# A fused S4D convolution and gated unit: eight pace units less ahead of the chunks, 4.4 per chunk, and transfers moved between queues

## The chip, the cores and the metric

The kernel runs on one core of one Trainium2 chip. A core has a matrix engine (TensorE, PE in the profile), a vector engine (DVE), a scalar engine (ACT), GpSimd (POOL) and SyncE (SP), each with its own list of instructions that it works off in order, and 16 DMA engines that all queues share. The metric is the device time of one execution in microseconds; a version's time is the median of its runs.

## The reference

The input u has 2048 tokens of 448 values. It is normalised once, and the result goes two ways; their sum with u is the output:

```python
xn = layernorm(u)
# state space convolution
A = -exp(log_A_real) + 1j * A_imag          # 448 x 256 modes
P = exp((A * dt[:, None])[:, :, None] * pos)
K = 2.0 * einsum("dn,dnl->dl", C * dt, P).real
y = irfft(rfft(xn.T, 2 * L) * rfft(K, 2 * L))[:, :L].T + xn * D_skip
# gated unit
h = sigmoid(xn @ w_gate) * (xn @ w_up)      # 448 -> 1792
out = u + y + h @ w_down                    # 1792 -> 448
```

All data are float32. The gated unit's matmuls work on values that are split in a high and a low part, so that each product is three matmuls (high by high, high by low, low by high).

## The kernel before, in words

**Two streams.** The program is written by two Python generators that run in turns while it is built: `conv()` for the convolution and `glu()` for the gated unit. Each yields a number of units of work, and the driver at the end of the file always continues the one with the smaller share done of its `total`. The constants at the top are these units: `WP` and `WX` for the preparation, `AHEAD` once before the chunks, `WK` for a chunk (given out in three parts), `HOLE` behind the chunks, `WS` for a step of the spectra. So they set how much of the gated unit is written between two pieces of the convolution. From the first step of the spectra on, the two take strict turns (`turns`) at each yield. A scheduler then places the instructions on the engines' lists, by the order written and by its own model of time; `tc.issue_after(x)` keeps an instruction behind `x`, if both are on the same engine, and does nothing to one on another engine. `sp_mm` and `glu_mm` hold the last matmul of each stream, so that with `issue_after` the matmuls of the spectra and of the gated unit stand on PE in the order in which they were written.

**The convolution.** 56 chunks of 8 channels each make the convolution's kernel K out of the modes. In each, four loads bring a phase table on SP (L483, `ph`), PE spreads it (L533, `tr`), ACT takes the sine of it (L541 to L544, `S`), POOL makes the modes' factors (L511, `me`, `mf`), DVE multiplies (L602 to L604, `Et`, `Ft`), and PE sums over the modes in 64 matmuls (L618, `ko`). Every four chunks a first stage of the transform (L559) goes to a buffer in DRAM (`sk_d`). The first stage of the tokens' own transform goes to DRAM as `x_d` (L279, in `x1_store`).
The spectra are 17 steps. A forward step (`there`, L891) multiplies both first stages by a table on PE into `pk` and `px`; DVE adds and subtracts (L898), multiplies both spectra (`product`), adds again (`halves`, L912), and one turn later PE goes back (`back`, L926), ACT copies the result to `vt`, and DMAs write it to `v_d` and bring it back turned (`turned`, `vp`). `last` (L962) makes the last stage for two halves h of the columns and four quarters q of the tokens, DVE adds it to `acc`, and `out_end` writes finished rows of the output (L232).

**The gated unit.** The tokens are worked in two halves of 1024, each as two blocks t of 512; the 1792 inner columns in 14 blocks, taken in groups of three (two in the last). `gate` makes gate and up projection of one column block and one token block, 11 matmuls `gu` of 512 columns each (L709); ACT takes the tanh (`th`, L717), DVE multiplies (L720), ACT rounds to the high part `hh` (L725) and DVE makes the low part `hl` (L727). After a group, nine matmuls `po` (L812) for each of the four 128-token blocks b give its part of the output, and DVE adds it to `acc` (L817). The first half splits the weights and stores both parts in DRAM, the second loads them back (L771 on SP). In the last group of the first half (`cross`) the tokens of the second half are loaded, normalised and transposed, and `pair_first` makes the first stage of their transform: ACT copies it (L693), and four stores for each pair of token blocks put it into `x_d`. At its end `acc` goes to `acc_d` (L832), and `acc` is loaded afresh with u for the second half (L236, on ACT's queue):

```python
if half == 1:
    for q in (2, 3):
        accs.append(acc_tile())
        x_load(accs[q], 4 * q, 4, [nc.scalar])
```

Of the last group of the second half, the block (t, b) = (0, 1) and all behind it are held back (`yield None`) until the convolution has written its last back step. What is left of `po` then stands between that and the last stage, except for the blocks of t = 1 with b above `LASTS`, which stand behind it.

Of the kernel before, what the change touches and what calls it, by code (L numbers as in the profile page):

```python
# [20 lines left out]
D = 448  # L21
# [5 lines left out]
TWO_PI = 2.0 * math.pi  # L27
MAGIC = 1.5 * 2.0**23
NFT = F // 128
WK = 4.83  # L30
WS = 5
HOLE = 6
AHEAD = 34
WP = 5
WX = 2
HELD = 9
LASTS = 1
HP = 300
Y0 = (8, 1)
CP = D // 4  # L40
# [86 lines left out]
def s4d_glu_kernel(ctx, tc, io):  # L127
    nc = tc.nc
# [556 lines left out]
    def pair_first(b, xns):  # L685

        x1 = pg.tile([128, 2, D], F32, name="x1", tag="wraw", bufs=1)
        pss = [psg.tile([128, 512], F32, name="gu", bufs=4) for _ in range(4)]
        for g in range(4):
            x_first_stage(pss[g][:, :D], xns, g)  # L690
        for g in range(4):
            to = x1[:, g] if g < 2 else pg.tile([128, D], F32, name="x1", tag="rd", bufs=RB)
            nc.scalar.copy(to, pss[g][:, :D])  # L693
            x1_store(row(b, g), to, nc.scalar)

    def gate(w, xs, to, between=None):
        wh, wl = w
# [32 lines left out]
    def glu():  # L730
        stores, later = [], []
        for half in range(2):
            if half == 1:
                for q in (2, 3):
                    accs.append(acc_tile())
                    x_load(accs[q], 4 * q, 4, [nc.scalar])
            for fs_ in ORDER[half]:
                fc, f0 = len(fs_), fs_[0]
                wts, ws, hs = [], [], [[], []]
# [12 lines left out]
                for n_, (f, t) in enumerate(order):  # L752
                    if t == 0:
                        wh = pg.tile([128, 2, 4, 128], F32R, name="wh", bufs=2)
                        if half == 0:
                            first = len(raws) == 2
                            raw, rd = raws.pop()
                            wl = w_low()
                            with hp(HP):
                                nc.scalar.copy(wh, raw)  # L760
                                if first:
                                    v.scalar_tensor_tensor(wl, raw, lim[:, 0, 0:1], wh, ALU.mult, ALU.subtract)
                                else:
                                    v.tensor_tensor(wl, raw, wh, ALU.subtract)
                            if not raws and f + 1 < NFT:
                                raws.append((w_load(f + 1), None))
                            stores.extend(kept((wh, wl), wt_d, f))
                        else:
                            wl = w_low()
                            for t_, d_ in kept((wh, wl), wt_d, f):  # L770
                                nc.sync.dma_start(t_, d_)  # L771
                        ws.append((wh, wl))
                    between = (lambda s_=mid[n_]: step(*s_)) if cross and mid[n_] else None
                    yield from gate(ws[f - f0], xq[2 * half + t], hs[t], between)
                    for t_, d_ in stores:
                        nc.sync.dma_start(d_, t_)
                    stores[:] = later
                    later.clear()
                    if t == 0:
                        dh = pg.tile([128, D], F32R, name="dh", bufs=FCH[0])  # L780
                        if half == 0:
                            rd = rd or rd_load(f)
                            dl = d_low()
                            with hp(HP), tc.issue_after((act if f == 1 else marks)[0].ins):
                                nc.scalar.copy(dh, rd)
                            nc.gpsimd.tensor_tensor(dl, rd, dh, ALU.subtract)
                            later.extend(kept((dh, dl), dt_d, f))
                        else:
                            dl = d_low()
                            for t_, d_ in kept((dh, dl), dt_d, f):  # L790
                                nc.sync.dma_start(t_, d_)
                        wts.append((dh, dl))
                    yield 2.5
                    for s_ in end[n_] if cross else ():
                        step(*s_)
                    if cross:
                        yield 2
                for t in range(2):
                    acc = accs[2 * half + t]
                    for b in range(4):  # L800
                        if final and (t, b) == (0, 1):

                            yield None
                        bs = slice(128 * b, 128 * b + 128)
                        end_ = final and (t, b) == (1, 3)
                        for h, ds in enumerate((slice(0, H), slice(H, D)) if end_ else (slice(0, D),)):
                            po = psg.tile([128, D], F32, name="po", tag="gu", bufs=4)
                            n = 0
                            with tc.issue_after(sp_mm[0].ins) if glu_on else nullcontext():
                                for (hh, hl), (dh, dl) in zip(hs[t], wts):  # L810
                                    for a_, w_ in ((hh, dh), (hh, dl), (hl, dh)):
                                        glu_mm[:] = [nc.tensor.matmul(  # L812
                                            po[:, ds], a_[:, bs], w_[:, ds], start=(n == 0), stop=(n == 3 * fc - 1)
                                        )]
                                        n += 1
                            with hp(HP):
                                v.scalar_tensor_tensor(  # L817
                                    acc[:, b, ds], po[:, ds], 0.5, acc[:, b, ds], ALU.mult, ALU.add
                                )
                            if final and t == 1 and b > 1:  # L820
                                out_end(acc[:, b : b + 1], 12 + b, ds)
                        if final and (t, b) == (1, LASTS):
                            sp_mm[:] = glu_mm
                            for q in range(4):
                                lasts[0](1, q)
                        if final and (t, b) == (1, 1):
                            out_end(acc[:, 0:2], 12, slice(0, D))
                        yield 0.6 * fc
                        if cross and (t, b) in downs:
                            step(*downs[t, b])  # L830
                    if cross:
                        nc.sync.dma_start(acc_d[:, 4 * t : 4 * t + 4], acc)  # L832

    def spectra(pf):
# [119 lines left out]
        def last(h, q):  # L954
# [15 lines left out]
                a = acc[:, p::2, ds]  # L970
                v.tensor_tensor(a, a, half(pb[q % 2][:, p, : 2 * H]), ALU.add)
            if h == 1 and q < 3:
                out_end(acc, 4 * q, slice(0, D), *([[nc.gpsimd]] if q == 0 else []))

        ac = acl[0]
        vts = [pf.tile([128, 4, H], F32, name="vt", bufs=2) for _ in range(2)]
# [57 lines left out]
        back(*made)  # L1034
        sp_mm[:] = glu_mm
        turned(*made[:2], 8, nc.gpsimd)
        back(*made_, (nc.sync, nc.scalar))
        turned(*made_[:2], 8)

# [141 lines left out]
```

## Time and profile before

| | |
|---|---|
| median of three runs | 724.4 us (723.02 to 726.36) |
| profiled execution, its own time | 727.67 us |
| its span | 725.9 us, mean granted clock of PE 0.96 |
| PE busy | 659.1 us, 91% of the span |
| DVE busy | 575.6 us, 79% |
| ACT busy | 420.3 us, 58% |
| POOL busy | 351.6 us, 48% |
| moved by DMA | 125.76 MB, 173 GB/s over the span |

A profile is one execution, recorded by the hardware. Busy time counts an engine's work but not the instructions that only issue DMAs or wait. The granted clock is TensorE's clock as a share of full speed. In a row of the timeline, what stands in brackets is the idle time ahead of an instruction and what ended it; an engine with a q behind its name (ACTq, SPq) is its queue of DMA issues. In a row of a groups view, out<-in is followed by the count, the busy time and the mean time of one in ns.

### The profile page before, as it was taken

How to read it: one execution, taken by the hardware profiler on the slowest of the kernel's cores; microseconds unless marked ns; L12 is line 12 of the kernel's file. 1: busy time of each engine (PE TensorE's matmuls, PEld its weight loads, DVE VectorE, ACT ScalarE, POOL GpSimd, SP SyncE). 2: the span in 40 equal slices, each digit the busy share in tenths (PEclk: the TensorE clock that was granted, in tenths of full speed). 3: DMA queues.
4: the chain of work that ended last, by engine and by line, in shares of the span. 5: the costliest groups of instructions: out<-in, count | busy, mean ns of one | idle time of the engine just before them, and what ended most of it. 6: DMA issues, size and time to landing. Idle time of an engine off the chain costs nothing.

```text
span 725.9 us, 20720 instructions
## 1 busy us (share of the span) xinstructions
PE 659.1 (91%) x8581; PEld 509.7 (70%) x8581; DVE 575.6 (79%) x779; ACT 420.3 (58%) x651; POOL 351.6 (48%) x395
## 2 busy tenths in 40 slices
PE   2798999999999899988979999999989999999784
PEld 1675788877778677655857887887776677777463
DVE  5689998699878798986548978897747989886823
ACT  3635455686678879996468768876822342332300
POOL 2111006785887879995335585686403224321101
PEclk9899999999899999999989999999989999999876
DMA  9977749645126454553962342433469787874456
GB/s 207 263 230 218 204 158 289 217 167 178 40 77 190 123 143 127 147 143 89 259 166 76 97 120 72 119 83 101 132 173 373 235 283 248 280 234 158 145 162 203
DMA packets 93630, 125.76 MB, mean 173 GB/s; under 512 B 12784, under 2 KB 79536, under 8 KB 93280
## 3 DMA queue, kind: packets, MB, share of 16 engines
q1 hardware_dynamic: 72000, 107.15, 46.9%
q10 hardware_dynamic: 20816, 14.91, 8.6%
q0 software_dynamic: 720, 2.36, 1.3%
q8 instruction: 68, 1.11, 0.6%
q14 instruction: 26, 0.21, 0.1%
HBM read 72.09 MB, written 52.30 MB: 171 GB/s over the span
## 4 chain that ended last, share of the span: by engine, by line
PE 49%; DVE 19%; DMA 10%; ACT 10%; issue 5%; POOL 3%; ACTq 1%; SPq 1%; DVEq 0%; POOLq 0%
PE gu L709 21%; PE po L812 13%; DVE Et L602 4%; DVE Ft L604 4%; DVE Et L603 3%; PE ko L618 3%; POOL me L511 2%; PE pk L891 2%; PE tr L533 2%; DMA x_d<-x 2%; PE px L891 2%; ACT S L544 2%; ACT S L541 2%; PE pk L926 1%; ACT S L542 1%
## 5 line engine op out<-in xcount | busy, mean ns | idle before, releaser
L511 POOL TENSOR_TENSOR me<-me,pm 128x32 f32<-128x32 f32 (+1 forms) x168 | 134.5, 801 | 97.3 <-DVE Et L603 85.1
L511 POOL TENSOR_TENSOR mf<-mf,pm 128x64 f32<-128x64 f32 (+1 forms) x112 | 121.0, 1080 | 5.8
L709 PE MATMUL gu<-xh,wh 128*128 128x512 f32 x336 | 103.5, 413 | 4.1 <-ACT xh L216 4.0
L603 DVE TENSOR_TENSOR Et<-me,S 128x1024 f32<-128x1024 f32 x56 | 79.2, 1414 | 23.0 <-ACT me L524 20.6
L709 PE MATMUL gu<-xh,wl 128*128 128x512 f32 x336 | 96.1, 392 | 0.0
L709 PE MATMUL gu<-xl,wh 128*128 128x512 f32 x336 | 95.9, 391 | 0.0
L812 PE MATMUL po<-dh,hh 128*128 128x448 f32 (+1 forms) x227 | 87.8, 387 | 2.9 <-DVE acc L817 1.4
L812 PE MATMUL po<-dh,hl 128*128 128x448 f32 (+1 forms) x227 | 84.9, 376 | 0.0
L725 ACT CAST hh<-gu 128x512 fp32r<-128x512 f32 x56 | 33.0, 590 | 89.3 <-DVE gu L720 82.5
L812 PE MATMUL po<-dl,hh 128*128 128x448 f32 (+1 forms) x227 | 84.6, 373 | 0.0
L604 DVE TENSOR_TENSOR Ft<-mf,S 128x1024 f32<-128x1024 f32 x56 | 78.3, 1399 | 7.5 <-POOL mf L511 3.9
L602 DVE TENSOR_TENSOR Et<-me,S 128x1024 f32<-128x1024 f32 x56 | 75.6, 1351 | 8.3 <-ACT S L544 7.9
L709 PEld LDWEIGHTS gu<-xh,wh 128*128 128x128 f32 x336 | 61.6, 193 | 26.6 <-issue 7.6
L618 PE MATMUL ko<-Et,Ft 128*32 128x64 f32 x3584 | 65.0, 224 | 12.4 <-DVE Ft L604 12.1
L618 PEld LDWEIGHTS ko<-Et,Ft 128*32 128x32 f32 x3584 | 54.8, 112 | 30.5 <-DVE Ft L604 16.8
L817 DVE SCALAR_TENSOR_TENSOR acc<-po,acc 128x448 f32<-128x448 f32 (+1 forms) x81 | 48.5, 609 | 33.0 <-PE po L812 33.0
L709 PEld LDWEIGHTS gu<-xh,wl 128*128 128x128 f32 x336 | 62.9, 188 | 14.6 <-DVE hl L727 0.7
L709 PEld LDWEIGHTS gu<-xl,wh 128*128 128x128 f32 x336 | 62.9, 188 | 14.2 <-issue 0.7
L541 ACT ACTIVATE S<-tr 128x1024 f32<-128x1024 f32 x56 | 57.9, 1034 | 25.7 <-PE tr L533 15.6
L907 POOL TENSOR_TENSOR yy<-yy 128x448 f32<-128x448 f32 (+1 forms) x16 | 23.5, 1471 | 92.7 <-DVE yy L904 92.7
L544 ACT ACTIVATE S<-S,hpi 128x1024 f32<-128x1024 f32 x56 | 65.9, 1176 | 0.1
L542 ACT ACTIVATE S<-tr 128x1024 f32<-128x1024 f32 x56 | 57.8, 1032 | 0.0
(204 smaller groups left out, 1268.1 us busy)
## 6 DMA issues: line engine op xcount, KB each, us to landing
wt_d<-wh SPq DMA_DIRECT2D x14, 512.0 KB
wt_d<-wl SPq DMA_DIRECT2D x14, 512.0 KB
sk_d<-sk ACTq DMA_DIRECT2D x28, 256.0 KB
wl<-wt_d SPq DMA_DIRECT2D x14, 512.0 KB
wh<-wt_d SPq DMA_DIRECT2D x14, 512.0 KB
sx<-x_d SPq DMA_DIRECT2D x16, 448.0 KB
skl<-sk_d SPq DMA_DIRECT2D x16, 448.0 KB
vp<-v_d SPq DMA_DIRECT2D x7, 896.0 KB
```

Of the source, the lines that this page charges most:

```text
L511: ins = nc.gpsimd.tensor_tensor(m[:, :, w + a : 2 * w : n], m[:, :, a:w:n], par(base + i).unsqueeze(2).to_broadcast([128, 4 * DC, w // n]) ...
L541: nc.scalar.activation(rows(cs), pv, AF.Abs)
L542: nc.scalar.activation(rows(S[:, 0:5:4]), pv, AF.Sin, scale=TWO_PI)
L544: sins[:] = [nc.scalar.activation(cs, cs, AF.Sin, scale=-TWO_PI, bias=hpi)]
L602: v.tensor_tensor(Et[:, :, :, 32:64], two(me[:, :, 32:64]), S[:, 1::-1], ALU.mult)
L603: v.tensor_tensor(Et[:, :, :, 0:32], two(me[:, :, 0:32]), S[:, 1:3, :, ::-1], ALU.mult)
L604: fts[:] = [v.tensor_tensor(Ft, two(mf), S[:, 3:5], ALU.mult)]
L618: nc.tensor.matmul(ko[32 * j : 32 * j + 32, sl], Ft[:, cc, DC * h + 4 * q + j], Et[:, cc, DC * h + 4 * q + j], start=(k == 0), stop=(k == ...
L709: glu_mm[:] = [nc.tensor.matmul(ps, a_, b_, start=(n == 0), stop=(n == len(mm) - 1))]
L725: nc.scalar.copy(hh, hf)
L812: glu_mm[:] = [nc.tensor.matmul(po[:, ds], a_[:, bs], w_[:, ds], start=(n == 0), stop=(n == 3 * fc - 1))]
L817: v.scalar_tensor_tensor(acc[:, b, ds], po[:, ds], 0.5, acc[:, b, ds], ALU.mult, ALU.add)
```

## The change

- `AHEAD` goes from 34 to 26 and `WK` from 4.83 to 4.4. The convolution's total is then 453.4 units instead of 485.5, the gated unit's stays at 413.4.
- `LASTS` goes from 1 to 2: of the last four `po` blocks, three instead of two stand ahead of the last stage, and their rows are written in one call.
- The stores of `pair_first` go from ACT's queue to SP's.
- The loads of the second half's `acc` go from its start to places behind its second and fourth projection, with `issue_after(marks[1])`; `marks[1]` is DVE's product of that projection. They stay on ACT's queue.
- `last` writes the first half of the columns of quarters 0 and 1 as soon as they are added (on SP), and at the end only the second half of these.
- Between the last two back steps one more turn is given to the gated unit.

```diff
--- before.py
+++ after.py
@@ -27,14 +27,14 @@
 TWO_PI = 2.0 * math.pi
 MAGIC = 1.5 * 2.0**23
 NFT = F // 128
-WK = 4.83
+WK = 4.4
 WS = 5
 HOLE = 6
-AHEAD = 34
+AHEAD = 26
 WP = 5
 WX = 2
 HELD = 9
-LASTS = 1
+LASTS = 2
 HP = 300
 Y0 = (8, 1)
 CP = D // 4
@@ -691,7 +691,7 @@
         for g in range(4):
             to = x1[:, g] if g < 2 else pg.tile([128, D], F32, name="x1", tag="rd", bufs=RB)
             nc.scalar.copy(to, pss[g][:, :D])
-            x1_store(row(b, g), to, nc.scalar)
+            x1_store(row(b, g), to, nc.sync)
 
     def gate(w, xs, to, between=None):
         wh, wl = w
@@ -733,7 +733,6 @@
             if half == 1:
                 for q in (2, 3):
                     accs.append(acc_tile())
-                    x_load(accs[q], 4 * q, 4, [nc.scalar])
             for fs_ in ORDER[half]:
                 fc, f0 = len(fs_), fs_[0]
                 wts, ws, hs = [], [], [[], []]
@@ -790,6 +789,10 @@
                             for t_, d_ in kept((dh, dl), dt_d, f):
                                 nc.sync.dma_start(t_, d_)
                         wts.append((dh, dl))
+                    if half == 1 and fs_ is ORDER[1][0] and n_ in (1, 3):
+                        q = 2 + n_ // 2
+                        with tc.issue_after(marks[1].ins):
+                            x_load(accs[q], 4 * q, 4, [nc.scalar])
                     yield 2.5
                     for s_ in end[n_] if cross else ():
                         step(*s_)
@@ -817,14 +820,13 @@
                                 v.scalar_tensor_tensor(
                                     acc[:, b, ds], po[:, ds], 0.5, acc[:, b, ds], ALU.mult, ALU.add
                                 )
-                            if final and t == 1 and b > 1:
+                            if final and t == 1 and b > LASTS:
                                 out_end(acc[:, b : b + 1], 12 + b, ds)
                         if final and (t, b) == (1, LASTS):
                             sp_mm[:] = glu_mm
                             for q in range(4):
                                 lasts[0](1, q)
-                        if final and (t, b) == (1, 1):
-                            out_end(acc[:, 0:2], 12, slice(0, D))
+                            out_end(acc[:, : LASTS + 1], 12, slice(0, D))
                         yield 0.6 * fc
                         if cross and (t, b) in downs:
                             step(*downs[t, b])
@@ -970,7 +972,9 @@
                 a = acc[:, p::2, ds]
                 v.tensor_tensor(a, a, half(pb[q % 2][:, p, : 2 * H]), ALU.add)
             if h == 1 and q < 3:
-                out_end(acc, 4 * q, slice(0, D), *([[nc.gpsimd]] if q == 0 else []))
+                out_end(acc, 4 * q, ds if q < 2 else slice(0, D), *([[nc.gpsimd]] if q == 0 else []))
+            elif h == 0 and q < 2:
+                out_end(acc, 4 * q, ds, [nc.sync])
 
         ac = acl[0]
         vts = [pf.tile([128, 4, H], F32, name="vt", bufs=2) for _ in range(2)]
@@ -1034,6 +1038,8 @@
         back(*made)
         sp_mm[:] = glu_mm
         turned(*made[:2], 8, nc.gpsimd)
+        yield WS / 2
+        sp_mm[:] = glu_mm
         back(*made_, (nc.sync, nc.scalar))
         turned(*made_[:2], 8)
```

**PE at the end of the spectra.** `gu` is the gated unit's projection, `po` its output product, the rows with `skl` and `sx` a forward step, those with `xx` a back step. Before, from the last but one forward step:

```order
L891 MATMUL pk<-skl,tb 32x224 x16
L891 MATMUL px<-sx,tb 32x224 x16
L926 MATMUL pk<-xx,bk 64x224 x8
L926 MATMUL px<-xx,bk 64x224 x8
L891 MATMUL pk<-skl,tb 32x224 x16
L891 MATMUL px<-sx,tb 32x224 x16
L926 MATMUL pk<-xx,bk 64x224 x8
L926 MATMUL px<-xx,bk 64x224 x8
L926 MATMUL pk<-xx,bk 64x224 x8
L926 MATMUL px<-xx,bk 64x224 x8
L926 MATMUL pk<-xx,bk 64x224 x8
L926 MATMUL px<-xx,bk 64x224 x8
```

After, from the last forward step:

```order
L893 MATMUL pk<-skl,tb 32x224 x16
L893 MATMUL px<-sx,tb 32x224 x16
L709 MATMUL gu<-xh,wh 128x512 x3
L709 MATMUL gu<-xr,wh 128x512
L709 MATMUL gu<-xh,wl 128x512 x3
L709 MATMUL gu<-xr,wl 128x512
L709 MATMUL gu<-xl,wh 128x512 x3
L928 MATMUL pk<-xx,bk 64x224 x8
L928 MATMUL px<-xx,bk 64x224 x8
L709 MATMUL gu<-xh,wh 128x512 x3
```

Before, the two forward and four back steps that are left stand in a row; with the change eleven `gu` stand behind the last forward step and eleven more behind the back step after it; the last but one forward step has eleven `gu` on both sides of its back step as well, and nine `po` stand ahead of the last back step.

**ACT where the gated unit changes halves.** `x` is the first stage of a token pair, `ks` belongs to K, `S` is the sine of a chunk's phases, `th` and `hh` belong to a projection. Before:

```order
L693 COPY x_4068<-gu 128x448 x2
L279 DMA x_d<-x_4068 64x2x224 x4
L693 COPY x_4087<-gu 128x448
L693 COPY x_4091<-gu 128x448
L236 DMA acc<-in_A_u_dram 32x1792
L279 DMA x_d<-x_4087 64x2x224 x2
L279 DMA x_d<-x_4091 64x2x224 x2
L631 COPY ks<-ko 128x512
L236 DMA acc<-in_A_u_dram 32x1792 x3
L450 ACTIVATE pm_1155<-pm_1155,one 128x640
L541 ACTIVATE S_1152<-tr 128x2x2x256
```

After:

```order
L236 DMA acc<-in_A_u_dram 32x1792
L219 CAST xr<-gu 64x256
L524 ACTIVATE me_1177<-me_1177 128x32x16
L236 DMA acc<-in_A_u_dram 32x1792 x3
L541 ACTIVATE S_1179<-tr 128x2x2x256
L542 ACTIVATE S_1179<-tr 128x2x2x256
L543 ACTIVATE S_1179<-tr 128x512
L544 ACTIVATE S_1179<-S_1179,hpi 128x2x512
L440 ACTIVATE pm_1235<-W_110,one 128x128
L717 ACTIVATE th<-gu 128x512
L236 DMA acc<-in_A_u_dram 32x1792 x4
L725 CAST hh<-gu 128x512
```

The stores `x_d<-x` are gone from ACT's list. The first four loads of `acc` still stand in front of a chunk's `S`; the second four stand in one row behind a `th`, where two, one and one stood apart before.

**SP at the same place,** after. `ph` are the four phase loads of a chunk, `acc_d` the store of the first half's sum:

```order
L483 DMA ph_1187<-phu_d 16x2x256
L483 DMA ph_1187<-phh_d 16x2x256
L483 DMA ph_1187<-phv_d 32x2x256
L834 DMA acc_d<-acc 128x1792
L483 DMA ph_1188<-phu_d 8x2x256
L279 DMA x_d<-x_4128 64x2x224 x2
L483 DMA ph_1188<-phu_d 16x2x256
L279 DMA x_d<-x_4128 64x2x224 x2
L279 DMA x_d<-x_4147 64x2x224 x2
L279 DMA x_d<-x_4151 64x2x224 x2
L483 DMA ph_1188<-phh_d 16x2x256
L483 DMA ph_1188<-phv_d 32x2x256
```

Before, none of the rows with `x_d` stood on this list here; now four rows of them stand among the phase loads.

## The prediction

> **What bounds the kernel now.** I began with the windows view, one row for each stage, to see where TensorE (PE) is short of work, then followed the chain of waits through the end, and looked at single instructions only where those two showed idle time.
>
> Windows view, by stage (start:end, length, busy time and count of each engine, granted clock, DMA share, GB/s):
>
> ```profile
> core 0: us, PE busy (x) PEld busy (x) DVE busy (x) ACT busy (x) POOL busy (x), PEclk, DMA share, GB/s
> 146.00:296.00 150.00, 139.96 (x2196) 113.26 (x2194) 133.88 (x144) 119.18 (x175) 118.76 (x122) 0.98 0.43 129
> 296.00:376.00 80.00, 68.43 (x950) 46.94 (x950) 55.98 (x69) 54.46 (x89) 47.30 (x56) 0.94 0.61 168
> 376.00:530.00 154.00, 151.05 (x2427) 123.44 (x2429) 128.96 (x135) 120.32 (x172) 99.34 (x119) 1.00 0.35 102
> 547.60:674.70 127.10, 125.55 (x1791) 90.31 (x1790) 108.23 (x158) 41.37 (x79) 38.80 (x30) 1.00 0.74 254
> 674.70:691.80 17.10, 12.83 (x257) 7.86 (x256) 14.17 (x22) 5.33 (x10) 3.11 (x2) 0.78 0.43 142
> 691.80:705.50 13.70, 10.60 (x52) 9.36 (x45) 3.12 (x5) 0.97 (x2) 0.52 (x1) 0.87 0.74 201
> 705.50:726.00 20.50, 10.40 (x155) 7.89 (x155) 6.02 (x11) 0.00 (x0) 1.98 (x4) 0.67 0.62 181
> ```
>
> The chunks run from 146 to 530. Late in them PE is busy 151.05 of 154 us while DVE has 128.96, ACT 120.32 and POOL 99.34: PE is the bound. The spectra up to 674.7 are the same (125.55 of 127.1). PE is short of work in three places: 296 to 376, where the gated unit changes halves; 674.7 to 691.8; and after 691.8.
>
> The chain of waits in the middle of the spectra gives the price of one slot (start, us, what):
>
> ```profile
> 585.20 2.77 PE gu L709 x11
> 589.01 2.72 PE gu L709 x11
> 591.74 0.92 PE pk L891 x32
> 592.65 0.76 PE px L891 x32
> 593.41 2.77 PE gu L709 x11
> 597.22 2.02 PE po L812 x9
> ```
>
> One projection (11 `gu` matmuls) is 2.75 us, so 0.25 each; one `po` block of nine is 2.02, so 0.224 each. A forward step (L891, both tiles) is 0.92 + 0.76 = 1.68. A back step (L926) fills 585.20 + 2.77 to 589.01, 1.04 us. No slot waits: while there is gated-unit work to put between steps, PE never stops.
>
> The same view's timeline of PE shows where that work runs out:
>
> ```profile
> 674.76 0.99 PE L891 MATMUL pk<-skl,tb 64*32 64x224 f32 x32
> 677.77 0.99 PE L926 MATMUL pk<-xx,bk 32*64 32x224 f32 x16 [1.27 <-DVE kk L898]
> 679.75 0.99 PE L891 MATMUL pk<-skl,tb 64*32 64x224 f32 x32
> 683.41 1.08 PE L926 MATMUL pk<-xx,bk 32*64 32x224 f32 x16 [1.92 <-DVE kk L898]
> 689.66 1.08 PE L926 MATMUL pk<-xx,bk 32*64 32x224 f32 x5 [1.00 <-DVE xx L912]
> 691.86 0.74 PE L812 MATMUL po<-dh,hh 128*128 128x448 f32 x1
> ```
>
> Two forward and four back steps are worth 2 x 1.68 + 4 x 1.04 = 7.5 us and take 691.86 - 674.76 = 17.1, because every step waits for DVE's adds and products of the one before. So 9.6 us of PE are unused there.
>
> **The change, part by part.** Counts are from PE's instruction lists, durations from the rows above.
>
> *Pace.* With 34 and 4.83 the shares of the two streams are 485.5 units against 413.4; with 26 and 4.4 they are 453.4 against 413.4. The gated unit reaches the first spectra step with 979 `gu` and 528 `po` matmuls done before, and 968 and 504 after. That is 11 x 0.25 + 24 x 0.224 = 8.1 us of PE moved out of the chunks. Bounds: 8.1 us if PE bounds every chunk; nothing if other engines do. In 304 of the 384 us it does, so I take 7.0: **-7.0**. The lists also bring the transposes of the preparation forward by up to 44 `gu`; DVE's list brings their inputs forward too, and I cost that at nothing (cover: PE has `gu` queued; if that is gone, I allow one wait of the size of the largest one that `ko` shows, the 4.79 us quoted below).
>
> *Spectra to 674.7.* Before, 253 `gu` and 81 `po` stand between the first forward step and the one at 674.76; after, 220 and 96. That is -33 x 0.25 + 15 x 0.224 = **-4.9**, all on PE.
>
> *The last two forward steps.* Now four projections and a `po` block stand among them: 4 x 2.75 + 2.02 = 13.0 us. With the steps' own 7.5 that is 20.5 against 17.1. They must also leave the chain on DVE covered. From the last forward step to the last back step it is 689.66 - 679.75 = 9.9 us now; the projections there add their own DVE work behind which it queues. Rows for that work, from the groups view:
>
> ```profile
> L817 DVE SCALAR_TENSOR_TENSOR acc<-po,acc 128x448 f32<-128x448 f32 (+1 forms) x81 | 48.5, 609 | 33.0 <-PE po L812 33.0
> L725 ACT CAST hh<-gu 128x512 fp32r<-128x512 f32 x56 | 33.0, 590 | 89.3 <-DVE gu L720 82.5
> ```
>
> I take three such DVE operations of 0.6, 1.8 us, so 11.7 us against 1.68 + 2 x 2.75 + 2 x 1.04 + 2.02 = 11.3 of PE work: 0.4 idle. The stretch becomes 20.9: **+3.8**. Bounds: +3.4 with all hidden, +13.0 if nothing is.
>
> *ACT's queue.* The stalls in 296 to 376, from ACT's timeline, one row of PE's, and two of the chain of waits:
>
> ```profile
> 344.67 4.41 ACTq L279 DMA_DIRECT2D x_d<-x  x4
> 349.12 0.53 ACT L693 COPY x<-gu 128x448 f32<-128x448 f32 x1 [3.98 <-DMA x_d<-x]
> 353.00 0.59 ACT L631 COPY ks<-ko 128x512 f32<-128x512 f32 x1 [2.91 <-DMA x_d<-x]
> 365.97 0.99 ACTq L236 DMA_DIRECT2D acc<-in_A_u_dram  x2
> 367.01 0.59 ACT L725 CAST hh<-gu 128x512 fp32r<-128x512 f32 x1 [6.64 <-issue]
> ...
> 369.50 1.93 PE L618 MATMUL ko<-Et,Ft 128*32 128x64 f32 x64 [4.79 <-DVE Ft L604]
> ...
> 353.53 4.15 DMA t<-in_c_t_dram
> 357.74 8.16 DMA acc_d<-acc
> ```
>
> The 32 stores of L279 leave ACT's queue, so the first two stalls (3.98 + 2.91) can go. PE had `po` and `gu` to do during them, so they are worth little. What PE lost is the 4.79 us at 369.5: ACT stood at a load of `acc` (L236) until the store `acc_d<-acc` had landed, the cast `hh` behind it was 6.64 late, and DVE's `Ft` behind that. The loads are written later now, but `issue_after(marks[1])` orders only instructions on DVE, where `marks[1]` runs; on ACT's list the second four still stand right behind the first `th`. So that stall stays. It can only shrink: the store no longer waits for the landing of `t` (4.15), and ACT reaches it earlier. Bounds: -4.8 to 0 for this; on the other side SP now queues phase loads behind the moved stores (rival D). I take half: **-2.5**.
>
> The Trainium skill speaks against this part: DMA: Bandwidth & Descriptors, "Issuing engines are not separate DMA queues", says that transfers from any engine share the same 16 DMA engines and that the choice saves only issue time. The row of 4.41 us for four issues agrees that a queue can be held, but not that PE gains; by the rule alone this term would be 0 and the sum 713.5 (rival F).
>
> *The end.* Chain of waits, SP's timeline, and windows of the output writes:
>
> ```profile
> 692.96 6.28 DMA v_d<-vt
> 699.26 6.15 DMA vp<-v_d
> 705.55 1.78 PE pk L962 x32
> 711.94 4.03 PE po L812 x27
> ...
> 711.83 11.82 SPq L232 DMA_DIRECT2D out_dram<-acc  x10
> ...
> 709.00:717.00 8.00, 6.96 (x95) 5.50 (x78) 4.87 (x9) 0.00 (x0) 1.95 (x4) 0.84 0.86 225
> 717.00:725.00 8.00, 0.00 (x0) 0.00 (x0) 0.00 (x0) 0.00 (x0) 0.00 (x0) 0.58 0.71 236
> ```
>
> The last combining stage (L962) starts 705.55 - 691.86 = 13.7 us after the last back step, set by the two DMAs. LASTS = 2 puts nine more `po` (2.0 us) into that wait, whose PE work ends at 702; it saves them after L962, where they no longer count either, because PE is done at 716 and the writes go on to 724.6 at 225 to 236 GB/s. Those writes are the whole output, 2048 x 448 x 4 = 3.67 MB. The change sends the first half of the columns of two of the four quarters early: 2 x 0.459 = 0.92 MB less, at 236 GB/s 3.9 us. Bounds: 0, if the end turns out to wait for the last issues and not for bandwidth, to 3.9. I take **-3.5**. The eight early writes stand on SP's list just ahead of the weights `wh`, `wl` of the last projection pair; those have four projections, 15 us, until they are needed, and SP is otherwise free there, so I cost them at nothing; with a landing like the 6 to 8 us above for both, they would be about 2 us late.
>
> Sum: -7.0 - 4.9 + 3.8 - 2.5 - 3.5 = -14.1. The profiled execution took 727.67 us, span 725.9; it becomes a span of 711.8. The median of the timed runs is 3.3 us under the profiled execution, so 724.4 - 14.1 = 710.3; I say **711**.
>
> **The rivals.**
> B: *the chunks do not shorten.* DVE is busy 133.88 of 150 in the first half of them; if its chain, not PE, sets the pace, the 7.0 fall away: 718. Against it stands 151.05 of 154.
> C: *the filled steps are serial.* If DVE's chain slips by as much as the work put in, +3.8 becomes +13.0: 720. For it: DVE is busy 14.17 of 17.1 there.
> D, *slower: SP becomes the queue that holds the chunks.* Its list now has stores of `x_d`, each waiting for a copy on ACT, ahead of and between the four phase loads of a chunk pair. A late phase load delays `S`, then `Et` and `Ft`, then `ko`. The price of one such miss is the 4.79 us row; at each of the four pairs 19 us, so 730. It decides once SP is more than one chunk pair late, about 13 us (384 / 56 x 2). Against it: the loads run a pair ahead, and 32 issues of some 0.6 us (4.41 and less for four) spread over 50.
> F: *ACT's relief buys nothing*, PE had work anyway: 713.5.
> G: *more than the sum:* the 4.79 us vanish wholly and PE enters L962 at full clock: 706.
>
> **How the numbers follow.** Forecast 0.45, F 0.15, B 0.13, C 0.09, D 0.11, G 0.07. A measurement here tells about 0.5%, 3.6 us, from no change, so "faster" is below 720.8. The forecast, F and G nearly always fall there (0.62 of 0.67), B mostly (0.09 of 0.13), C about half the time (0.04): 0.75. Same, 720.8 to 728: the rest of these, 0.14. Slower: D, 0.11. The range reaches from G's far side, 702, to past C, 723; D and a little at either edge stay out.
>
> **What would show it.** Right: the first L893 step (was L891) near 540 in place of 547.7; no wait over 1 us on L928 in the last two steps, and a granted clock near 1.0 there; last L964 to the end of the span about 3.5 us shorter; the wait before `ko` near 369 below 4.79. Wrong: waits of `tr` or ACT's `S` on `ph` loads (D); chunk intervals unchanged with PE idle between (B); L928 still waiting on L898 or L912 with `gu` around it (C); `gu` waiting for `wl` or `wh` late in the spectra.

## The result and the profile after

The changed kernel takes 713.6 us (median of 4 runs, 712.46 to 714.46) where the kernel before took 723.7 beside it: a ratio of 0.987, 95% interval 0.984 to 0.990. The forecast was 711, its range 702 to 723; the gain was 10.1 us where 13 to 14 were forecast. The profiled execution after took 714.46 us, span 712.7. (Of one experiment, pace and ACT's queue together, the profiled execution was a disturbed one; neither its time nor its stages are used.)

The windows view of the changed kernel, cut at the same events as the one of before: start of the chunks, the change of halves, end of the chunks, first forward step, last but one forward step, end of the last back step, last stage (start:end, length, busy time and count of each engine, granted clock, DMA share, GB/s):

```profile
core 0: us, PE busy (x) PEld busy (x) DVE busy (x) ACT busy (x) POOL busy (x), PEclk, DMA share, GB/s
...
367.70:519.10 151.40, 149.33 (x2484) 121.88 (x2484) 129.70 (x134) 119.80 (x171) 101.61 (x116) 1.00 0.36 105
519.10:531.70 12.60, 9.07 (x104) 7.76 (x105) 3.79 (x6) 2.30 (x4) 0.54 (x1) 1.00 0.75 221
531.70:662.90 131.20, 127.06 (x1772) 89.51 (x1772) 103.25 (x156) 38.70 (x74) 46.25 (x30) 0.95 0.80 265
662.90:684.30 21.40, 20.89 (x311) 14.88 (x310) 17.68 (x27) 7.91 (x16) 3.13 (x2) 1.00 0.42 130
684.30:695.50 11.20, 11.17 (x60) 10.06 (x57) 3.12 (x5) 0.68 (x2) 0.51 (x1) 1.00 0.72 206
695.50:712.70 17.20, 6.24 (x146) 4.73 (x146) 5.78 (x11) 0.00 (x0) 2.22 (x4) 0.81 0.54 162
```

Three things stand there. The last two forward and four back steps (662.9 to 684.3) keep PE busy for 20.89 of 21.40 us at full clock, as forecast. The last stage to the end is 17.2 us in place of 20.3. And the spectra up to the last but one forward step take 131.2 us in place of 127.1, although they hold 4.9 us less of matmuls; their granted clock is 0.95 where it was 1.00. The place is at their start:

```profile
531.70:537.70 6.00, 5.46 (x98) 3.41 (x99) 3.70 (x6) 1.89 (x4) 0.24 (x1) 0.72 1.09 336
537.70:543.70 6.00, 5.58 (x82) 3.84 (x80) 5.90 (x10) 1.30 (x3) 2.95 (x2) 1.00 1.02 408
543.70:549.70 6.00, 3.48 (x21) 2.48 (x22) 5.93 (x10) 0.53 (x1) 3.09 (x2) 0.68 1.01 384
549.70:555.70 6.00, 5.35 (x83) 2.60 (x81) 2.18 (x4) 1.06 (x2) 2.27 (x2) 0.50 0.76 217
```

PE's timeline of the changed kernel at that place:

```profile
531.69 1.29 PE L893 MATMUL pk<-skl,tb 64*32 64x224 f32 x32 [2.86 <-DMA skl<-sk_d]
...
538.56 0.36 PE L815 MATMUL po<-dh,hh 128*128 128x448 f32 x1
...
546.22 1.77 PE L928 MATMUL px<-xx,bk 32*64 32x224 f32 x16 [2.89 <-issue]
...
549.21 0.57 PE L815 MATMUL po<-dh,hh 128*128 128x448 f32 x1
...
552.88 1.75 PE L893 MATMUL pk<-skl,tb 64*32 64x224 f32 x32 [0.65 <-ACT vt L934]
554.37 1.75 PE L893 MATMUL px<-sx,tb 64*32 64x224 f32 x32
556.05 0.99 PE L709 MATMUL gu<-xh,wh 128*128 128x512 f32 x3
```

PE stands for 2.89 us ahead of the first back step, while DVE is busy for 5.93 of 6 us. From 546.2 to 556.05 it then runs at half its clock: a `po` matmul takes 0.57 in place of 0.36, half a forward step 1.75 in place of 0.99. Of those 9.8 us 0.65 are idle, and half of the rest, 4.6, is lost; with the two waits it is 8.1.

What the back step waits for stands in DVE's timeline of the same kernel. It writes `px`, the tile from which DVE still reads the forward step before it, until 545.51 + 0.60 = 546.11, 0.11 us ahead of the back step:

```profile
545.51 0.60 DVE L900 TENSOR_TENSOR xx<-px,oo 128x448 f32<-128x448 f32 x1
```

PE's first back step in the kernel before:

```profile
562.43 0.98 PE L926 MATMUL pk<-xx,bk 32*64 32x224 f32 x16 [0.15 <-issue]
```

Counted from the first forward step, the back step starts 14.75 us later before (562.43 - 547.68) and 14.53 us later after (546.22 - 531.69). So the start that DVE sets comes at the same time in both. The kernel before had 33 `gu`, 8.25 us of PE, to put between; the changed one has 18 `po`, 4.0 us.

### The profile page after: what moved, and what is told of

It is laid out like the page before. It is cut to its first block, busy times and chain, and to the rows that moved or that the text cites. A ratio compares the mean times of both kernels' runs of the same rounds, so it can differ in the third digit from the quotient of the medians.

```text
span 712.7 us, 20746 instructions
## 1 busy us (share of the span) xinstructions
PE 657.0 (92%) x8581; PEld 505.9 (71%) x8581; DVE 575.8 (81%) x779; ACT 418.1 (59%) x651; POOL 375.9 (53%) x395
## 5 line engine op out<-in xcount | busy, mean ns | idle before, releaser
L511 POOL TENSOR_TENSOR me<-me,pm 128x32 f32<-128x32 f32 (+1 forms) x168 | 145.6, 867 | 65.5 <-DVE Et L603 52.4
L604 DVE TENSOR_TENSOR Ft<-mf,S 128x1024 f32<-128x1024 f32 x56 | 79.7, 1424 | 12.9 <-PE ko L618 5.6
L909 POOL TENSOR_TENSOR yy<-yy 128x448 f32<-128x448 f32 (+1 forms) x16 | 31.1, 1941 | 99.0 <-DVE yy L906 99.0
L709 PEld LDWEIGHTS gu<-xh,wh 128*128 128x128 f32 x336 | 60.0, 190 | 26.9 <-issue 8.7
L541 ACT ACTIVATE S<-tr 128x1024 f32<-128x1024 f32 x56 | 58.1, 1038 | 35.5 <-PE tr L533 21.8
L709 PEld LDWEIGHTS gu<-xh,wl 128*128 128x128 f32 x336 | 63.0, 188 | 14.6 <-DVE fr L305 0.7
L720 DVE SCALAR_TENSOR_TENSOR gu<-th,gu 128x512 f32<-128x512 f32 x56 | 38.5, 688 | 27.5 <-PE gu L709 11.5
```

The costliest lines, as they stand in the source:

```text
L511: ins = nc.gpsimd.tensor_tensor(m[:, :, w + a : 2 * w : n], m[:, :, a:w:n], par(base + i).unsqueeze(2).to_broadcast([128, 4 * DC, w // n]) ...
L541: nc.scalar.activation(rows(cs), pv, AF.Abs)
L604: fts[:] = [v.tensor_tensor(Ft, two(mf), S[:, 3:5], ALU.mult)]
L709: glu_mm[:] = [nc.tensor.matmul(ps, a_, b_, start=(n == 0), stop=(n == len(mm) - 1))]
L720: marks[1] = v.scalar_tensor_tensor(hf, th, 1.0, pgu[1], ALU.add, ALU.mult)
```

## The experiments

Call P the pace, A the moves around ACT's queue (stores to SP, `acc` loads later), and E the end (LASTS, early half writes, the extra turn). E1 to E3 do one part alone on the kernel before, E5 to E7 take one part back from the changed kernel.

**E1, the pace alone.** Against the kernel before:

```diff
-WK = 4.83
+WK = 4.4
...
-AHEAD = 34
+AHEAD = 26
```

> The kernel before with AHEAD 26 and WK 4.4 alone (no store, load or output write is moved, LASTS stays 1, no turn is added). Theory P (the prediction's): the pace carries most of the change, -7.0 in the chunks and -4.9 in the spectra, +3.8 in the last steps: 723.7 - 8.1 = 715.6. Theory Q (from the profile after): the chunks gain only the 6.8 us of matmuls moved out, the spectra cost 4.1 and the last steps 4.3 more, the wait behind them 2.5 less: 723.7 - 0.9 = 722.8, and the 8 us of waits that went from the chunks come back, the 4.8 us wait of ko on Ft at the change of halves among them.

Measured: 722.56 us, ratio 0.9988 (0.9953 to 1.0024). Theory Q was right in the sum: alone, the pace that was to bring most of the gain brings nothing that can be measured. Its chunks are shorter; the spectra pay it back. PE's first back step, in its timeline:

```profile
538.16 1.75 PE L890 MATMUL pk<-skl,tb 64*32 64x224 f32 x32 [4.78 <-DMA skl<-sk_d]
...
553.98 1.40 PE L925 MATMUL pk<-xx,bk 32*64 32x224 f32 x12 [3.69 <-issue]
```

The same wait stands here as in the changed kernel, so it comes with the pace. Q also had the 4.8 us wait of `ko` come back; it did not (see E2).

**E2, ACT's queue alone.**

```diff
-            x1_store(row(b, g), to, nc.scalar)
+            x1_store(row(b, g), to, nc.sync)
...
-                    x_load(accs[q], 4 * q, 4, [nc.scalar])
...
+                    if half == 1 and fs_ is ORDER[1][0] and n_ in (1, 3):
+                        q = 2 + n_ // 2
+                        with tc.issue_after(marks[1].ins):
+                            x_load(accs[q], 4 * q, 4, [nc.scalar])
```

> The kernel before with its stores of pair_first on SP's queue and the two x_load calls behind the second and fourth projection, nothing else. Theory P (F in the prediction at its zero): -2.5, 721.2, or 723.7 if PE had work anyway. Theory Q: all of the waits in the chunks that the change removed were ACT's queue, -5 to -8: 716 to 719. Slower than before would mean that SP now holds the phase loads.

Measured: 722.7 us, 0.9979 (0.9947 to 1.0011), between 0.8 us slower and 3.8 faster: the 5 to 8 us of theory Q are out. ACT's timeline shows why so little came of it:

```profile
353.45 0.60 ACT L717 ACTIVATE th<-gu 128x512 f32<-128x512 f32 x1
361.14 0.81 ACTq L236 DMA_DIRECT2D acc<-in_A_u_dram  x2
361.99 0.58 ACT L725 CAST hh<-gu 128x512 fp32r<-128x512 f32 x1 [7.94 <-issue]
```

PE's timeline of the same kernel has the wait that follows from it:

```profile
364.48 1.54 PE L618 MATMUL ko<-Et,Ft 128*32 128x64 f32 x64 [4.03 <-DVE Ft L604]
```

The second four loads stand behind a `th` and still hold ACT until `acc_d` has landed; the cast `hh` behind them is 7.94 us late, and `ko` waits 4.03. In the changed kernel the same cast is 9.54 late, but `ko` waits for only 0.98, and in the kernel with the pace alone (E1) no `ko` between 340 and 385 us waits for more than 0.49. With the old pace it still waits for 3.65 (E3) and 3.36 us (E7, below), so this wait goes with the pace. The two rows of the changed kernel, one from ACT's timeline and one from PE's:

```profile
365.16 0.59 ACT L725 CAST hh<-gu 128x512 fp32r<-128x512 f32 x1 [9.54 <-DMA acc<-in_A_u_dram]
...
367.66 1.10 PE L618 MATMUL ko<-Et,Ft 128*32 128x64 f32 x64 [0.98 <-DVE Ft L604]
```

**E3, the end alone.** Against the kernel before:

```diff
-LASTS = 1
+LASTS = 2
...
-                out_end(acc, 4 * q, slice(0, D), *([[nc.gpsimd]] if q == 0 else []))
+                out_end(acc, 4 * q, ds if q < 2 else slice(0, D), *([[nc.gpsimd]] if q == 0 else []))
+            elif h == 0 and q < 2:
+                out_end(acc, 4 * q, ds, [nc.sync])
...
+        yield WS / 2
+        sp_mm[:] = glu_mm
         back(*made_, (nc.sync, nc.scalar))
```

> The kernel before with LASTS 2, the early half writes and the extra turn, nothing else. The pace of before leaves the last steps without projections, so the extra turn has nothing to bring. Theory P: the tail is bound by the bandwidth of the writes, 0.92 MB less: -3.5, 720.2. Rival: the tail is bound by the number of writes that are issued last; 16 in place of 20 of them: -3 as well, but the DMA rate in the last 5 us stays far under the 236 GB/s. If neither, 723.7. LASTS alone should be worth nothing here if the wait for vp sets the last stage (13.7 us between last back step and last stage stays).

Measured: 719.65 us, 0.9954 (0.9922 to 0.9985). From the last stage to the end it takes 16.7 us where the kernel before takes 20.3; from the last back step to the last stage 13.2 where that took 13.7, so nothing much comes of LASTS here (its share was not run by itself).

**E4, more work at the start of the spectra.** Against the changed kernel:

```diff
             glu_on[:] = [1]
             yield WS / 2
+            if n in (1, 2):
+                yield WS / 2
```

> The changed kernel with one more turn of the gated unit between the forward and the back step of the second and third step of the spectra, so that 18 + 6 po and 11 gu stand before the first back step where 12 + 6 po stood. Theory Q: the 3.3 us wait near 543 and the half clock for some 10 us after it come from too little work there; both go, worth about 8; the work is missing at the end, where one forward and three back steps stand bare again, +5: 713.6 - 3 = 710.6, with the spectra shorter by 6 or more up to the last but one forward step. Rival: the wait near 543 is that for loads while the DMA engines are busy all the time (405 GB/s); then it stays and the end costs 5: 718.6.

Measured: 711.97 us, 0.9851 (0.9791 to 0.9911). PE's timeline, first back step and the forward step behind it, and DVE's last read of `pk` ahead of them:

```profile
548.50 0.61 DVE L900 TENSOR_TENSOR kk<-pk,oo 128x448 f32<-128x448 f32 x1
...
549.22 0.98 PE L928 MATMUL pk<-xx,bk 32*64 32x224 f32 x16 [0.20 <-issue]
550.33 0.99 PE L928 MATMUL px<-xx,bk 32*64 32x224 f32 x16
553.96 0.99 PE L893 MATMUL pk<-skl,tb 64*32 64x224 f32 x32
```

The wait is 0.20 in place of 2.89, and the clock stays full there, though the DMA engines are as busy as before. More work on PE would cover a wait for a load just as well, so this alone does not tell the two apart; the trace does: here too the back step starts 0.11 us behind DVE's read (549.11). PE had too little to do while DVE worked; it did not wait for a load. Less its `gu` and `po`, the stretch up to the last but one forward step takes 47.3 us; it is 54.7 in the changed kernel and 45.7 before (129.3 - 82.0, 131.2 - 76.5, 127.1 - 81.4, at 0.25 and 0.224 us each). By this account 7.4 us are the price of the bare start. The kernel as a whole gains only about 1.6, within the noise, because 22 `gu` fewer are left at the end: the last steps take 20.5 us in place of 21.4 with 5.5 us less work in them, and the wait behind them 12.8 in place of 11.2.

**E5, E6 and E7, two parts at a time:** the changed kernel with A taken back, with E taken back, with P taken back (the diffs of E2, E3 and E1 in reverse).

> The changed kernel with the stores of pair_first back on ACT's queue and the acc loads back at the start of the second half: pace and end together. Alone the parts gave -0.8 (pace), -0.7 (ACT's queue), -3.8 (end), 5.3 of 10.1. Theory X: the missing 4.8 come from pace and end together (the turn given at the end needs the projections that the pace brings there): 714.3. Theory Y: they come from pace and ACT's queue together (fewer matmuls in the chunks show ACT's waits, and their removal then pays): 718.9, with waits of ko on Ft or of tr on S at the change of halves.

> The changed kernel with LASTS 1, whole writes at the end and no extra turn: pace and ACT's queue together. Theory X: 721.9, last stage 12.6 us or more after the last back step. Theory Y: 717.1, the chunks end some 5 us earlier than with the pace alone.

> The changed kernel with AHEAD 34 and WK 4.83: ACT's queue and end together. Both theories: 723.4 - 0.7 - 3.8 = 718.9. Markedly less (714) would say that the pace does nothing at all in this company.

Measured: P and E 716.98 us, 0.988 (0.983 to 0.993); P and A 718.99, 0.9939 (0.991 to 0.997); A and E 719.24, 0.9952 (0.993 to 0.998). In us by these ratios:

| parts | gain | parts | gain |
|---|---|---|---|
| P | 0.9 | P, E | 8.7 |
| A | 1.5 | P, A | 4.4 |
| E | 3.3 | A, E | 3.5 |
| none | 0 | all | 9.4 |

P is worth 5.4 and 5.9 with E beside it and 0.9 and 2.9 without. That leans to theory X, an interaction of pace and end, but it does not settle it. Each gain in the table is uncertain by 1.7 to 3.8 us, and the mean difference of 3.7 by some 3.3 (the intervals taken as independent). In times, theory X had 714.3 and theory Y 718.9 for P and E, and 721.9 and 717.1 for P and A; both measurements, 716.98 and 718.99, lie between the two. A adds little where E is there (0.2, 0.7), and 3.5 beside P alone.

The stages of the profiles repeat better, except for the chunks. Lengths in us, between the events of the windows above:

| kernel | chunks | to first forward step | to last but one forward step | to last back step | to last stage | to the end |
|---|---|---|---|---|---|---|
| before | 388.0 | 13.5 | 127.1 | 17.1 | 13.7 | 20.3 |
| A | 384.7 | 10.9 | 127.2 | 17.2 | 12.5 | 21.0 |
| E | 383.8 | 12.6 | 127.1 | 17.7 | 13.2 | 16.7 |
| A, E | 386.2 | 12.9 | 128.0 | 17.1 | 12.9 | 16.9 |
| P | 378.2 | 14.6 | 130.3 | 21.4 | 12.6 | 20.7 |
| P, E | 376.8 | 14.4 | 129.8 | 21.4 | 11.4 | 17.1 |
| all | 374.6 | 12.6 | 131.2 | 21.4 | 11.2 | 17.2 |
| E4 | 375.6 | 13.3 | 129.3 | 20.5 | 12.8 | 16.9 |

The chunks of four kernels with the pace of before differ by 4 us from one profile to the next; the spectra repeat within 1 us with the old pace and 1.5 with the new one, the last steps within 1 us.

Outside the chunks (the sum of the other five columns) the pace costs 7.9 us without E (P against before), and 6.8 and 5.8 with it. So these stages hold only 1 to 2 us of an interaction; the rest would have to lie in the chunks, where the noise is too large to see it. Some of it lies ahead of the last stage. The chain of waits of E1, from the end of its last back step:

```profile
689.89 12.70 PE po L812 x54
702.59 1.07 PE pk L961 x32
```

With the pace and without the extra turn, 54 `po` fill the wait ahead of the last stage and set its end; the extra turn takes nine of them to the other side of the last back step.

**E8, one write for the last rows.** Against the changed kernel:

```diff
-                            if final and t == 1 and b > LASTS:
-                                out_end(acc[:, b : b + 1], 12 + b, ds)
...
-                            out_end(acc[:, : LASTS + 1], 12, slice(0, D))
+                        if end_:
+                            out_end(acc, 12, slice(0, D))
```

> The changed kernel with the rows of the last quarter written by one call of four DMAs at the very end in place of three calls for them (one of blocks 0 to 2 and two for block 3, twelve DMAs). If the tail is bound by bandwidth: no change, or slower by up to 1 us since all of them start only when the last rows are done (702.6). If it is bound by the number of writes, each waiting for one that was issued eight earlier to land (in the profile after the last two are issued at 709.7 and 709.9, 7 us after their rows are ready): some 2 to 2.5 us faster, 711.3.

Measured: 712.41 us, 0.9874 (0.9841 to 0.9907). By the median this is not told apart from the changed kernel, but the tail is 15.4 us in place of 17.2. The windows of the changed kernel's tail, then SP's timeline there with two rows of its waits view (waited for: us in total, times, longest; L1183 is a helper's line), and SP's timeline of E8:

```profile
700.00:704.00 4.00, 2.20 (x19) 2.02 (x18) 2.02 (x5) 0.00 (x0) 0.38 (x1) 1.00 0.96 244
704.00:708.00 4.00, 0.00 (x0) 0.00 (x0) 0.00 (x0) 0.00 (x0) 0.00 (x0) 0.79 0.95 338
708.00:712.70 4.70, 0.00 (x0) 0.00 (x0) 0.00 (x0) 0.00 (x0) 0.00 (x0) 0.50 0.24 70
```

```profile
700.26 9.72 SPq L232 DMA_DIRECT2D out_dram<-acc  x8
...
SPq L232 <- DMA out_dram<-acc: 2.0, 4, 0.8
SPq L1183 <- DMA out_dram<-acc: 1.3, 4, 0.9
```

```profile
699.85 5.67 SPq L232 DMA_DIRECT2D out_dram<-acc  x4
```

In the changed kernel the last rows are added by 702.6, but SP issues its eight writes over 9.7 us, to 710.0: in the trace the later ones wait, 3.3 us in all, for the landing of writes issued earlier, whose semaphores they take over. In the last 4.7 us only 70 GB/s move. With four writes the issues end at 705.5. So this tail ends with writes that wait for one another. E12, with the same edit, has the same 15.4 us; E10, below, limits how far the number of writes counts.

**E9, without the early half writes,** and **E10, with LASTS 1.** Both against the changed kernel:

```diff
-                out_end(acc, 4 * q, ds if q < 2 else slice(0, D), *([[nc.gpsimd]] if q == 0 else []))
-            elif h == 0 and q < 2:
-                out_end(acc, 4 * q, ds, [nc.sync])
+                out_end(acc, 4 * q, slice(0, D), *([[nc.gpsimd]] if q == 0 else []))
```

```diff
-LASTS = 2
+LASTS = 1
```

> The changed kernel with the first two quarters written whole at the end again (0.92 MB more in the tail, the same number of writes). Bandwidth of the tail: 3.9 us more than the changed kernel, 717.5, with 20.5 to 21 us from the last stage to the end. Number of writes alone: under 1 us more.

> The changed kernel with LASTS 1: nine po go back behind the last stage and four more writes stand in the tail. If the last stage waits for the turned data, it starts at the same 11.2 us after the last back step and the tail is longer by the PE work behind it and one more half wave of writes, 1.5 to 2: 715.3. If it waits for the po ahead of it, it starts 2.0 earlier, and the sum is even: 713.6.

Measured: E9 715.87 us, 0.9884 (0.983 to 0.993), tail 20.4 us; E10 714.83 us, 0.9857 (0.980 to 0.992), tail 17.3 and 10.5 us ahead of the last stage. The early half writes carry 3.2 us of the tail (20.4 to 17.2) at the same number of writes behind the last stage. LASTS carries nothing that can be seen: in E10 the last stage starts 0.7 us sooner, where none or 2.0 was expected. E10's tail is no longer than 17.3 us, though SP and ACT issue twenty writes of `acc` in it in place of sixteen; the 1.5 to 2 us expected for these did not come. So a tail does not grow with each write more; only the step to the single last call in E8 showed. The chain of waits of E10:

```profile
686.51 4.39 DMA v_d<-vt
690.97 5.15 DMA vp<-v_d
696.26 1.13 PE pk L964 x32
```

The two DMAs end 10.3 us after the last back step, so the nine `po` that LASTS 2 puts in front make the last stage wait for PE, 0.7 us longer, as the changed kernel's chain shows:

```profile
684.32 11.14 PE po L815 x54
695.47 0.03 issue
695.49 1.13 PE pk L964 x32
```

**E11, both ends of the spectra filled.** E4's edit, and `WK = 4.2` in place of 4.4.

> The changed kernel with the two turns of e4 at the start of the spectra and WK 4.2, so that twelve po more go from the chunks into the spectra: before the first back step stand 18 + 12 po, and the end keeps its projections. In e4 the start of the spectra cost 7.4 us less, but the end had 22 gu less to cover its steps, 4.6 us and 1.6 at the wait behind them. If these are all, both ends filled give 713.6 - 7 = 706.6. Rival: the chunks below 4.4 units are bound by DVE and give nothing back, or the start waits for data at 400 GB/s: 710 to 713.

Measured: 713.43 us, 0.9851 (0.980 to 0.990), close to the rival's 710 to 713. The spectra take 128.1 us with 2.7 us more of matmuls than in the changed kernel, so their start was filled, and the last steps take 21.4. But the chunks and the stretch up to the first forward step together take 387.0 us where they took 387.2, with twelve `po` (2.7 us) less in them. One profile of the chunks is good to some 4 us only, so no gain shows there, and which engine held it is open.

**E12, E4 and E8 together,** at `WK = 4.4`.

> The changed kernel with the two turns of e4 and the one last write of e8, WK 4.4. Both act in stages that do not touch each other: e4 took the wait at the start of the spectra away and lost part of it at the end, 1.6 us by its median, e8 shortened the tail by 1.8 us in its profile and 1.2 by its median. Together 713.6 - 2.8 = 710.8, with 15.4 us from the last stage to the end and no wait over 2 us at the first back step. If the gain of either is noise: 712 to 713.6.

Measured: 712.81 us (6 runs), 0.9842 (0.9805 to 0.988), tail 15.4 and no wait at the first back step. 2.8 us were expected against the changed kernel and 0.8 is what the medians show; the interval overlaps that of the changed kernel, so no version was found that is shown to beat it.

## Why the prediction was right, and which of its steps were not

The time and its range were right; the sum came near by luck, since errors cancel in it. Its terms, with the means of the profiles that have or lack a part (stage table, E8 to E10 with those of the same pace):

- **Pace, -7.0.** With P the chunks go from 385.9 to 377.5 where A is not there (means of before and E, of P and P with E), 8.4 less; the stretch to the first forward step is 1.5 longer (13.0 to 14.5). That is -6.9, as forecast, but with two chunk lengths on each side that vary by 4 us the closeness is luck. (The forecast's own share, 304 of 384 us, of 8.1 would have been 6.4; 7.0 was a rounding up without a reason given.)
- **Spectra, -4.9.** This step failed. The stretch is 127.4 with the old pace (mean of four) and 130.5 with the new one (mean of P, P with E, all, E8, E9, E10): +3.2. I had read that no slot waits in the middle of the spectra and looked at the order only at their end. At their start the new pace puts 12 and 6 `po`, 4.0 us, ahead of the first back step where 22 and 11 `gu`, 8.25 us, stood. The step that failed is the reading that PE sets the time of every slot there: DVE sets when the first back step can start, 14.5 us after the first forward step, so the matmuls taken out of that place gave back no time. In the changed kernel's profile the stretch is +4.1, 9.0 off the forecast. PE's two waits there, 3.5 us, and the 4.6 lost at half clock make 8.1 of it. E4 takes 7.4 away by filling that place. Most of the rest is at the first two forward steps, which take 4.9 us before, 5.5 in the changed kernel and 6.0 in E4, at half clock for 3.4 us in the latter two.
- **Last two forward steps, +3.8.** 17.3 to 21.4 (means): +4.1. The steps were covered as reckoned, by the pace alone (E1 has 21.4 without the extra turn, with a wait of 2.53 us where nine `po` stand in the changed kernel). Rival C is out.
- **ACT's queue, -2.5.** Alone 1.5 by its ratio, with no effect that can be told from zero; beside the end 0.2 and 0.7, beside the pace without the end 3.5. The stage table has up to 4.8 for it beside the pace (chunks 377.5 to 374.4, to the first forward step 14.5 to 12.8, means with E8 to E10), but the chunks are noisy by that much. The size stays open between 0 and 5. What I said of the second four loads held: they still hold ACT (9.54 us late). The 4.79 us wait of `ko` went all the same, and not with A, which alone still had 4.03 of it (E2), but with the pace. F, which says that this relief buys nothing, is not excluded.
- **The wait ahead of the last stage, 0.** It went from 13.1 (mean of four with the old pace) to 11.2. I had taken it as given. LASTS did not do it (E10 has 10.5). Two things changed. The data come sooner: the last load of `vp` is issued 7.3 us after the last back step before (6.4 to 6.6 in E2, E3 and E7), 5.5 in the changed kernel, and 5.4 in E1, which has the pace and not the extra turn. So the extra turn is not needed for that; the projections that the pace brings to the last steps may be its cause (E4 has fewer of them, and 6.4). And it is no longer always the data that the last stage waits for: in E1, E4 and E12 54 `po` set it, for 12.7 to 13.0 us, the first of them at half clock; in the changed kernel they take 11.1. The extra turn without LASTS was run (E10), LASTS without the turn was not, so how the two share the 1.9 us is read, not shown.
- **The end, -3.5.** 20.7 (before, A, P) to 17.0: -3.7, of which E9 gives 3.2 to the early half writes. The bound of 0, for an end that waits for the last issues, had something in it: E8 gets another 1.8 from a single last call.

Sum of these: -6.9 + 3.2 + 4.1 - 4.8 - 1.9 - 3.7 = -10.0, with ACT's queue at its upper end, which is where the measured 10.1 lies. With ACT's queue at nothing it would be -5.2, so the parts taken one by one do not settle that term either.

Rival D did not happen: in the changed kernel's trace no wait of `tr` is put down to a phase load. (Its row of 4.41 us for four issues is 1.1 each, not the 0.6 for which it was quoted.) Both conditions of rival G came true, the wait of `ko` down to 0.98 and full clock up to the last stage, and the time did not follow, for the spectra. Rival B was wrong for `WK` 4.4; E11 fits it for 4.2, without showing that DVE sets the pace there. The profiled execution before, 727.67 us, was also among the longest of its kind (timed runs from 717 to 729 in the experiments), so 13.2 us between the profiles overstates what the medians show.

The page rule that I weighed against the ACT term, of the Trainium skill, DMA: Bandwidth & Descriptors, "Issuing engines are not separate DMA queues", gave F's 713.5; the measured 713.6 agrees with it only by sum, since the spectra missed by more.

## What to carry to other kernels

When work is shifted from one stage to another, look at every seam it passes, not only at the one that it is meant to fill: a stage in which no slot waits can be bare in its first steps, and a matmul that covers a gap at the end is missing at the start. Ask there which engine sets the time: work moved out of a place where another engine does gives nothing back. The pace measured 0.9 us alone and over 5 beside the end, with 2 to 4 us of uncertainty, so take parts away one at a time and in pairs before one of them is credited, and compare the spread before an interaction is believed. At a tail of writes, look at which writes wait for one another as well as at their bytes.

## What the runs showed of the hardware

A wait of 2.89 us was enough for PE to come back at half clock, and it stayed there for 9.8 us, with no wait over 0.65 us in them. That cost more (4.6 us) than the wait. The Trainium skill, TensorE: Matmul & The Clock Gate, "Part 1: The HAM clock gate", says that the clock is full again after some 3.4 us of sustained work. The granted clock in the fourteen traces agrees with that length as a step, but one step is often not the end of it: all 114 stretches at half clock, without the last of each trace, which runs past the end, are whole multiples of 3.41 us, 60 of them one, 44 two, 9 three and one four. The one behind the 2.89 us wait is three steps, 10.24 us; behind the 3.54 us wait ahead of the first forward step of E4 came one. What decides how many there are is not shown. A wait need not be as long as a step, either: in the kernel before, the clock fell to half at 684.2, with no wait over 1.92 us since the last but one forward step.

In the tail, 338 GB/s were reached for 4 us with many writes under way, and 70 GB/s for the last 4.7 us, in which the last four were issued behind waits for earlier ones.
